# Forty throwaway matmuls in place of forty-seven at the start of a spectral-filter-plus-MLP kernel

## The chip, the cores and the metric

The kernel runs on one core of one Trainium2 chip. The metric is the device time of one execution in microseconds; lower is better. Three runs of the kernel before gave 148.82, 148.93 and 149.20 us, so the median is 148.93 us.

## The reference, cut to what matters

One input `x` of 2048 rows and 640 columns (bf16) is layer-normalised along its columns. The normalised `xn` goes through two branches, and the output is their sum with `x`:

```
xn  = _layernorm(x, axis=-1)
X   = jnp.fft.rfft2(xn, axes=(-2, -1)) * (w_r + 1j * w_i)
y_A = jnp.fft.irfft2(X, s=(2048, 640), axes=(-2, -1))
y_B = gelu(xn @ w1 + b1) @ w2 + b2          # w1 640x1536, w2 1536x640
return x + y_A + y_B
```

## The kernel before, in words

The 2048 rows are cut into 16 row tiles of 128 rows (tile c holds every sixteenth row). Branch B is two layers of matmuls. Branch A is a two-dimensional Fourier transform written as matmuls with constant tables (`gtab`, `etab`, `mtab` and, on the way back, `ntab`, `getab`, `htab`), with foldings on VectorE (DVE) between them and the filter multiplication in the middle.

The program is a list of operations with buffers that they read and write. The order on every engine is written out by hand in the string `ORDER` (`K.arrange(ORDER)`), and `K.sync()` puts in the semaphore waits that the buffers demand. Each engine then runs its own list strictly in order. Neither the string nor the planner's cost estimates are computed again at build time, so a number of matmuls inside one operation can change without moving anything on any engine.

What the first 40 us hold, with the lines of the profile:

- SyncE (SP) issues the loads back to back (L375): row tiles 0 and 1 of `x` one by one, then three chunks of `w1` (into `W1`), `x` tiles 2 and 3, two more chunks of `w1`, the table `gtab`, the other `x` tiles in pairs, and `w2`. None of these issues waits for a compute engine.
- DVE zeroes a 128x128 tile `warm` (L399), and TensorE (PE) multiplies it by itself, writing into a PSUM bank that nobody reads. These are the throwaway matmuls. They are built by `idle(n, ...)` (L411 to L412, recorded under L383), called once with `WARM[0]` matmuls (L413) and once with `WARM[1]` (L532). In `ORDER` both calls stand at the head of PE's list, so they form one unbroken run.
- DVE takes the statistics of a row tile (L480, L482), and ScalarE (ACT, row tile 0, L486) or GpSimd (POOL, all others, L491) makes the reciprocal standard deviation `rstd` from `ve` (L490). DVE then normalises the tile into `T` (L510).
- PE transposes row tiles 0 to 3 against `ident` (L528, five 128x128 transposes each), and DVE (L395) and ACT (L394) copy them out of PSUM into `xnT`. Most later row tiles are transposed by DMAs that SP issues (L519), each of them waiting for DVE's L510.
- Between the transposes PE turns the bias `b1` into a column (twelve one-column matmuls, `ident,gT`) and then runs the first layer of branch B: 24 matmuls with chunks 0 and 1 of `w1` on tile 0, the transposes of tile 1, and so on. ACT applies the GELU (L593, L611).
- DVE folds the normalised tiles for branch A (L540, L544), and PE transforms them with `gtab`.

From then on PE carries the second layer, the Fourier stages and the output, in the order of `ORDER`.

Of the kernel before, what the change touches and what calls it, by code (L numbers as in the profile page):

```python
# [88 lines left out]
def mm_us(n):  # L89
    return max(n / 2400.0 + 0.0027, 0.0265)  # L90
# [6 lines left out]
def act_us(n, ptr=0):  # L97
    return 0.067 + n / 1200.0 + 0.078 * ptr
# [191 lines left out]
AHEAD = 2  # L290
CHAIN = "b0 b1 c00 c01 b2 c10 c11 d00 d01 b3 b4 c20 c21 d10 d11 b5 c30 c31 d20 d21 d30 d31".split()
XASPLIT = [((0, 1, 2, 3, 4),)] * 7 + [((0, 1), (2, 3, 4))]
WARM = (39, 8)
FILTER = {7: 4}


def bass_parallel_sum__spectral_gfnet__dense_activation_gelu__prompt_kernel(
# [21 lines left out]
    with ExitStack() as es:  # L319
# [45 lines left out]
        def psb(slot, dims, off=0, p0=0, n=128):  # L365
            return bass.AP(tensor=PS, offset=p0 * 4096 + slot * 512 + off, ap=[[4096, n]] + dims)
# [20 lines left out]
        def pe(segs, prio, lst, **kw):  # L387

            return K.op([("pe", sum(u for _, u in segs))], prio, mms(lst), segs=segs, **kw)
# [19 lines left out]
        def idle(n, us, **kw):  # L409

            b = Buf("warmps", psum)  # L411
            return pe([("128", us)], 300, lambda: [(psb(b.slot, [[1, 128]]), warm[:], warm[:], True, True) for _ in range(n)], reads=[B_warm], writes=[b], **kw)  # L412
        idle(WARM[0], 0.1067 * 32 + (WARM[0] - 32) * mm_us(128))  # L413

# [80 lines left out]
        for pair in range(8):  # L495
# [10 lines left out]
            for n in range(2):  # L506
# [15 lines left out]
                for j0, j1, engs in ((0, 2, ["dve"]), (2, 5, ["act"])) if c < 2 else ((0, 5, ["dve", "act"]),):  # L522
# [8 lines left out]
                    if j0 and not c:  # L531
                        idle(WARM[1], WARM[1] * mm_us(128), gate=[tp])  # L532
                    us = {"dve": 0.06 + 0.068 * nj, "act": act_us(128 * nj)}
# [287 lines left out]
```

## Time and profile before

| | us |
|---|---|
| median of three runs (148.82 to 149.20) | 148.93 |
| the profiled execution's own time | 149.58 |
| span of that execution, first to last instruction | 147.8 |
| PE busy | 141.9 (96%) |
| DVE busy | 110.0 (74%) |
| ACT busy | 72.3 (49%) |
| POOL busy | 21.5 (15%) |

The profile is of one execution; 149.58 - 147.8 = 1.8 us of its time lie outside the span. A row of a timeline reads: start, duration, engine, line, operation, output and inputs, shape, count, and in brackets the engine's idle time before it with what ended it. PE's matmuls overlap: the spacing of starts within a row of n matmuls is (duration of the row - duration of one) / (n - 1). A row of the chain of waits reads: start, duration, and what the chain was in.

### The profile page before, as it was taken

What the parts mean: (1) busy time and instruction counts of PE and PEld (TensorE: products, weight loads), DVE (VectorE), ACT (ScalarE), POOL (GpSimd) and SP (SyncE); (2) the same over time, 40 slices, a digit from 0 to 9 for tenths busy, and PEclk for the clock granted to TensorE, in tenths of its full rate; (3) what the DMA queues carried; (4) which work ended last, traced back from release to release, by engine and by line L of the source; (5) the groups of instructions that cost most, each with busy time, mean ns of one, the idle gap of its engine ahead of it and who ended that gap; (6) DMA issues with size and microseconds to landing.
All of it is one profiled execution on the core that took longest, in us unless ns stands there. A gap on an engine that the chain in (4) does not pass through costs nothing.

```text
span 147.8 us, 3951 instructions
## 1 busy us (share of the span) xinstructions
PE 141.9 (96%) x1677; PEld 90.5 (61%) x1692; DVE 110.0 (74%) x240; ACT 72.3 (49%) x118; POOL 21.5 (15%) x35
## 2 busy tenths in 40 slices
PE   7999999999799999999999999999999999999993
PEld 7999995655456645445644545555666656655573
DVE  2688999999996367856966979864099787769543
ACT  3615995047598579977775756121075400430000
POOL 1002040301200005000000000000002024545620
DMA  5999999569999998988700670475302107777974
GB/s 119 305 402 399 378 388 132 113 141 135 165 163 160 158 161 218 350 334 45 141 4 0 41 138 10 89 93 106 71 4 24 20 4 84 93 89 91 114 87 114
DMA packets 29843, 21.01 MB, mean 142 GB/s; under 512 B 20225, under 2 KB 27137, under 8 KB 29826
## 3 DMA queue, kind: packets, MB, share of 16 engines
q1 hardware_dynamic: 27232, 15.84, 49.7%
q0 software_dynamic: 2592, 4.92, 17.8%
q8 instruction: 13, 0.21, 0.6%
q14 instruction: 4, 0.03, 0.1%
q10 hardware_dynamic: 2, 0.00, 0.0%
HBM read 13.54 MB, written 5.24 MB: 127 GB/s over the span
## 4 chain that ended last, share of the span: by engine, by line
PE 89%; DVE 5%; DMA 2%; issue 2%; SPq 1%
PE ps L383 88%; DMA xnT<-T 2%; DVE W L780 1%; DVE stats L480 1%; PE ps L528 1%; DVE T L544 1%; DVE T L510 1%; DVE T L540 1%; DVE X L771 1%; SPq L519 1%; DVE mv L482 0%; DVE warm L399 0%; DVE ve L490 0%
## 5 line engine op out<-in xcount | busy, mean ns | idle before, releaser
L383 PE MATMUL ps<-xnT,W 128*128 128x512 bf16 (+2 forms) x336 | 56.9, 320 | 1.0 <-DMA xnT<-T 1.0
L383 PE MATMUL ps<-W,gT 128*128 128x128 bf16 (+3 forms) x382 | 55.0, 292 | 1.5 <-issue 1.0
L383 PEld LDWEIGHTS ps<-W,gT 128*128 128x128 bf16 x396 | 30.1, 98 | 22.5 <-issue 1.7
L383 PEld LDWEIGHTS ps<-xnT,W 128*128 128x128 bf16 x336 | 31.4, 114 | 18.5 <-ACT gT L611 2.8
L611 ACT ACTIVATE gT<-ps,b1col 128x512 bf16<-128x512 f32 (+1 forms) x48 | 28.4, 638 | 15.1 <-PE ps L383 15.1
L787 POOL DMA_DIRECT2D out_dram<-W x14 | 12.3, 990 | 71.0 <-DVE W L780 71.0
L394 ACT ACTIVATE Wf<-ps 128x960 bf16<-128x960 f32 (+1 forms) x10 | 8.5, 888 | 17.9 <-PE ps L383 17.9
L480 DVE BATCH_NORM_STATS2 stats<-X 128x6 f32<-128x320 bf16 x32 | 14.0, 477 | 2.1 <-DMA X<-in_A_x_dram 2.1
L678 DVE TENSOR_TENSOR T<-Y,Wf 128x1288 bf16<-128x1288 bf16 x16 | 12.5, 822 | 0.0
L491 POOL TENSOR_TENSOR rstd<-ve,mhalf 128x2 f32<-128x2 f32 (+1 forms) x8 | 6.0, 744 | 31.9 <-DVE ve L490 31.8
L395 DVE CAST Y<-ps 128x644 bf16<-128x644 f32 x7 | 5.8, 829 | 5.4 <-PE ps L383 5.4
L394 ACT ACTIVATE Xb<-ps 128x960 bf16<-128x960 f32 (+1 forms) x7 | 8.0, 1166 | 3.4 <-PE ps L383 3.3
L544 DVE TENSOR_TENSOR T<-T 128x512 bf16<-128x512 bf16 (+1 forms) x32 | 9.0, 313 | 0.2
L394 ACT ACTIVATE XV<-ps 128x1280 bf16<-128x1280 f32 (+2 forms) x8 | 8.9, 1109 | 0.5 <-PE ps L383 0.5
L395 DVE CAST Xb<-ps 128x960 bf16<-128x960 f32 (+1 forms) x5 | 5.5, 1105 | 4.2 <-PE ps L383 4.2
L394 ACT ACTIVATE Y<-ps 128x644 bf16<-128x644 f32 x9 | 6.3, 708 | 4.1 <-PE ps L383 4.0
L510 DVE TENSOR_SCALAR T<-X,mv,rstd 128x640 bf16<-128x640 bf16 x16 | 6.9, 441 | 1.5 <-POOL rstd L491 1.0
L383 PE MATMUL ps<-getab,XV 32*128 32x160 bf16 (+1 forms) x128 | 7.5, 242 | 0.0
L540 DVE TENSOR_TENSOR T<-T 128x640 bf16<-128x640 bf16 x16 | 7.4, 480 | 0.1
L739 DVE TENSOR_TENSOR Wf<-Wf 128x960 bf16<-128x960 bf16 (+1 forms) x12 | 6.7, 596 | 0.9 <-PE ps L383 0.8
L780 DVE TENSOR_TENSOR W<-ps,b2bc 128x640 bf16<-128x640 f32 x6 | 4.8, 821 | 3.3 <-PE ps L383 3.3
L383 PE MATMUL ps<-etab,XV 32*128 32x160 bf16 (+1 forms) x128 | 7.2, 232 | 0.0
(53 smaller groups left out, 123.1 us busy)
## 6 DMA issues: line engine op xcount, KB each, us to landing
out_dram<-in_A_x_dram POOLq DMA_DIRECT2D x4, 640.0 KB, 7.3
X<-in_A_x_dram SPq DMA_DIRECT2D x7, 320.0 KB, 9.4
out_dram<-W POOLq DMA_DIRECT2D x14, 160.0 KB, 3.4
W<-in_B_w_dram SPq DMA_DIRECT2D x5, 384.0 KB, 5.8
W<-in_B_w_dram SPq DMA_DIRECT2D x3, 640.0 KB, 12.8
Wf<-in_A_w_r_dram SPq DMA_DIRECT2D x7, 160.5 KB, 3.9
Wf<-in_A_w_i_dram SPq DMA_DIRECT2D x7, 160.5 KB, 4.6
gtab<-c_G SPq DMA_DIRECT2D x1, 512.0 KB, 9.1
```

Of the source, the lines that this page charges most:

```text
L383: ins = e.matmul(o_, lhsT=lw, rhs=rh, start=st, stop=sp_, skip_group_check=True)
L394: return e.activation(dst(), src(), ACT.Copy, scale=scale)
L395: return e.tensor_copy(dst(), src())
L480: st_ops.append(K.op([("dve", 0.393)], pr, lambda e, _, c=c, h=h: e.bn_stats(stats[:, c, 6 * h:6 * h + 6], view(X, c * D + H2 * h, [[1, H2 ...
L510: o = K.op([("dve", 0.356)], pr, lambda e, _, c=c, n=n, xnv=xnv: e.tensor_scalar(out=xnv(n, 0, [[1, D]]), in0=view(X, c * D, [[1, D]]), sc ...
L540: K.op([("dve", 0.39)], pr, lambda e, _, k=k, op=op, xnv=xnv, x1v=x1v: e.tensor_tensor(out=x1v(H2 * k, [[D, 2], [1, H2]]), in0=xnv(0, 0, [ ...
L544: ring_ops.append(K.op([("dve", 0.333 if w == 128 else 0.136)], pr, lambda e, _, op=op, x1v=x1v, xfv=xfv, o_=o_, o0=o0, o1=o1, w=w: e.tens ...
L611: K.op([("act", act_us(128 * nt, 1) + 0.02)], pr + PRIO["gelu"], lambda e, _, c0=c0, nt=nt, fc=fc, hps=hps: e.activation(gT[:, fc, 128 * c ...
L678: filt_ops.append(K.op([("dve", 0.738)], pr, lambda e, _, k=k, Y=Y, TB=TB, pair=pair: e.tensor_tensor(out=view(TT, TB.slot * 8 * KP + k * ...
L739: K.op([("dve", 0.068 + n / 6)], pr + 3, lambda e, _, k=k, op=op, y2=y2, yf=yf, n=n: e.tensor_tensor(out=view(Wf, YF + yf.slot * 3 * D + ( ...
L780: K.op([("dve", dve_us(w))], 95, lambda e, _, os_=os_, fps=fps, o0=o0, w=w, xo=xo, base=base: e.tensor_tensor(out=view(W1, OST + os_.slot ...
L787: last.append(K.op([("pool", 0.9)], 450, lambda e, _, c=c, os_=os_: e.dma_start(ov[:, c, :], view(W1, OST + os_.slot * D, [[1, D]]), accum ...
```

## The change

One constant changes: the first `idle` call issues 32 throwaway matmuls and no longer 39. With the 8 of the second call, PE's list begins with 40 of them and no longer 47. On every other engine, and behind the throwaway matmuls on PE, the instructions, their order and their waits are the same.

```
-WARM = (39, 8)
+WARM = (32, 8)
```

## The prediction

> **What bounds the kernel now.** I read the page's chain first, then the chain of waits in order of time, then PE's and DVE's timelines over the first microseconds, then single loads with their time to landing.
>
> The page's chain by engine says that PE sets the end:
>
> ```profile
> PE 89%; DVE 5%; DMA 2%; issue 2%; SPq 1%
> ```
>
> The chain in order of time (start, duration, what) shows where the head of PE's list matters, and where it stops mattering:
>
> ```profile
> 0.99 5.19 PE ps L383 x47
> 6.19 0.53 PE ps L528 x5
> ...
> 22.54 6.50 PE ps L383 x53
> 29.04 0.02 issue
> 29.06 0.07 DVE T L544
> ...
> 35.64 0.80 SPq L519
> 36.44 0.04 issue
> 36.48 2.64 DMA xnT<-T
> 39.12 0.09 issue
> 39.21 23.83 PE ps L383 x268
> ```
>
> The 47 throwaways are its first large piece. At 29.04 it leaves PE for DVE, goes through a DMA transpose, and returns to PE at 39.21, where PE had waited. So what is won early counts only as far as DVE shares it. PE's and DVE's timelines at the head:
>
> ```profile
> 0.99 5.19 PE L383 MATMUL ps<-warm 128*128 128x128 bf16 x47 [0.99 <-DVE warm L399]
> 5.98 0.74 PE L528 MATMUL ps<-ident,T 128*128 128x128 bf16 x5
> 6.65 0.55 PE L383 MATMUL ps<-ident,gT 1*128 1x1 bf16 x12
> 7.13 1.53 PE L383 MATMUL ps<-xnT,W 128*128 128x128 bf16 x24
> 8.50 0.44 PE L528 MATMUL ps<-ident,T 128*128 128x128 bf16 x5
> ```
> ```profile
> 4.72 0.45 DVE L510 TENSOR_SCALAR T<-X,mv,rstd 128x640 bf16<-128x640 bf16 x1
> ```
>
> Tile 0 is normalised at 4.72 + 0.45 = 5.17, but its transposes start at 5.98, right behind the throwaways. One throwaway lasts 0.314 us, so their starts are (5.19 - 0.31) / 46 = 0.106 us apart. The first transposes: (0.74 - 0.31) / 4 = 0.107. The 24 real matmuls, at 0.22 us each: (1.53 - 0.22) / 23 = 0.057. So PE ran at half its rate until between 6.4 and 7.1, the granted clock reading 1.00 throughout. All 47 throwaways ran slow.
>
> **The change, part by part.** *Removed:* 7 x 0.1065 = 0.75 us of PE. Tile 0 becomes usable at 5.17 plus a hand-over of about 0.07 (the DVE copy's signal at 7.06 is followed by PE's row at 7.13), so the transposes start at about 5.25 instead of 5.98: 0.73 us earlier. The 40 slow throwaways end just then, and PE does not idle.
>
> *What follows at once.* DVE waited 0.94 us for these transposes (its copy at 6.75). That copy moves to 6.02, and behind it in DVE's queue the `ve` of tile 1, POOL's `rstd` and the normalising of tile 1 (7.79 to about 7.06). All are 0.73 earlier; nothing else is in their way.
>
> *What stops it on PE.* Loads do not move: SP's issues wait for no compute engine. The first three `w1` chunks are issued at 1.66, 2.13 and 2.61 and land 4.8, 5.3 and 5.8 us later: 6.5, 7.4 and 8.4. PE uses them at 7.13, 7.8 (twelve matmuls further on) and 8.78. With about 0.1 us to pick each up, the lead shrinks to 0.5, 0.3 and 0.28 us. I take 0.28 us for PE from there on.
>
> *What stops it on DVE.* The statistics of tiles 2 and 3, now at 9.42, need a load issued at 3.08 that takes 6.2: it lands at about 9.27, so DVE's lead is at most 0.13 there. DVE idles 0.09 us before its copy at 13.69 and can regain that. Then comes the load that decides: its issue, its landing (last number), and the DVE instruction that needs it, each from its own answer:
>
> ```profile
> 6.68 0.71 SPq L375 DMA_DIRECT2D X<-in_A_x_dram  x1
> ```
> ```profile
> X<-in_A_x_dram SPq DMA_DIRECT2D x1, 320.0 KB, 9.4
> ```
> ```profile
> 16.13 0.49 DVE L480 BATCH_NORM_STATS2 stats<-X 128x6 f32<-128x320 bf16 x1
> ```
>
> 6.68 + 9.4 = 16.1: DVE starts on it as it lands. Whatever lead DVE had is spent, and from 16.1 to 29 it is packed. One hole is left, just where the chain leaves PE:
>
> ```profile
> 28.77 0.14 DVE L490 TENSOR_SCALAR ve<-mv 128x2 f32<-128x2 f32 x1
> 29.06 0.43 DVE L544 TENSOR_TENSOR T<-T 128x512 bf16<-128x512 bf16 x1
> ```
>
> The hole is 29.06 - 28.91 = 0.15 us, and DVE instructions otherwise overlap by a few hundredths, so DVE can start up to about 0.2 us earlier if PE is 0.28 earlier. PE has no wait of its own between 13 and 29 that would eat that lead (it idles 0.05 there). From 29.06 the chain is DVE, SP's issue, the DMA and PE, each waiting for the one before it, so 0.15 to 0.2 goes through to 39.21 and to the end. The lead PE holds beyond it becomes idle time before 39.21, which hides it.
>
> *Sum.* I take -0.18 us: 149.58 to 149.4 for the profiled execution. That one lies 0.65 above the median; carried over, 148.93 - 0.18 = 148.75 us. Bounds: 0 if the hole at 29 does not close, or if PE in other executions speeds up before its throwaways are over and they end earlier anyway; -0.73 if no load were in the way.
>
> *The unknown cost: what the throwaways buy.* The trace shows that PE changes rate after some 5.7 us of nearly unbroken work (0.99 to about 6.7), not what decides the moment. Before, real transposes filled PE to 6.5 with a hole of 0.13. After, they end at 5.8, then twelve one-column matmuls run to about 6.35, then PE idles until chunk 0 has landed and is picked up at about 6.6. If the moment is fixed by time, or the work until 5.8 is enough, this costs nothing. If unbroken work is needed, the fast rate comes later: the second rival.
>
> [...]
>
> [...]
>
> **The rivals.** *Full rate comes later (slower).* Every microsecond at half rate costs PE 1 - 57/107 = 0.47 us of matmuls. PE begins its real matmuls about 0.5 us earlier, so the point of balance is about 1 us of delay, until 7.7. PE's row of transposes at 13.21 feeds DVE's copy at 13.69 with 0.09 us to spare, and behind that DVE is packed up to 35.6, so a late PE passes straight through to the end. If the change needs the same 5.7 us again from 6.6 on, it comes at 12.3, and the loss is 5.6 x 0.47 - 0.5 = 2.1 us; between that and nothing I take the middle, 1.1 us: 150.0 us. For it: PE stayed slow through 5.0 us of unbroken throwaways, so the condition is not met easily, and its new hole of 0.2 to 0.8 us lies just before 6.7. Against it: 4.8 us of unbroken work remain, and weight loads of 0.11 us each fill most of the one-column stretch.
>
> *The whole 0.73 us goes through (faster): 148.2 us.* The landings that stop it are those of one profiled execution, which was 0.65 us slower than the median. If the loads land some tenths earlier otherwise, DVE keeps more of its lead. Against it: the loads keep the DMA engines full in this stretch (9s in the page's slices), and several of them, not one, leave under 0.5 us.
>
> *It does not do what it says.* If PE usually changes rate before the throwaways end, fewer of them are slow and the removed ones cost little: 148.9. That lies within the forecast's case.
>
> **How the numbers follow.** About 0.3% (0.45 us) is what a measurement of this kernel can tell from no change. Forecast: 0.44, at 148.5 to 149.0; all of it counts as the same. Late full rate: 0.36, at 149.4 to 151.0. Full lead: 0.20, at 148.1 to 148.5. So faster 0.20, same 0.44, slower 0.36. The range 148.2 to 150.1 leaves out the upper part of the second case (0.13) and the edge of the third (0.05).
>
> **What would show it.** Right: transposes (L528) at about 5.25, the copy behind them at about 6.0, the 24 matmuls at about 6.6 and still 0.056 apart, DVE's statistics at 16.1 unmoved, the return to PE at about 39.0. Wrong by the second rival: the 24 matmuls 0.107 apart, and DVE's copy at 13.69 and its statistics at 16.13 later by the same amount. Wrong by the third: the statistics at 16.13 earlier.

## The result, and the profile after

The change makes the kernel slower by 0.9%: the ratio of its time to that of the kernel before is 1.0092, with a 95% interval of 1.0064 to 1.0119. That is 148.88 us before (median of six runs) and 149.74, 150.22, 150.53 and 150.59 us after. Left out of all ratios are runs more than 1.5% above the fastest of their kernel: two of the change (152.0 and 152.3 us) and two of e2 below (152.2 and 152.4), each at a mean granted clock of 0.99, one each of e4 (150.6) and e9 (150.8) at 1.00, and one of the kernel before (207.6) at 0.66. The profiled execution took 150.53 us with a span of 148.7, against 149.58 and 147.8 before.

PE's timeline at the head of the kernel after (start, duration, operation, count):

```profile
0.99 4.23 PE L383 MATMUL ps<-warm 128*128 128x128 bf16 x40 [0.99 <-DVE warm L399]
5.28 0.45 PE L528 MATMUL ps<-ident,T 128*128 128x128 bf16 x5
5.66 0.55 PE L383 MATMUL ps<-ident,gT 1*128 1x1 bf16 x12
6.15 0.86 PE L383 MATMUL ps<-xnT,W 128*128 128x128 bf16 x12
7.86 0.86 PE L383 MATMUL ps<-xnT,W 128*128 128x128 bf16 x12 [0.85 <-DMA W<-in_B_w_dram]
8.56 0.44 PE L528 MATMUL ps<-ident,T 128*128 128x128 bf16 x5
```

The transposes start at 5.28, 0.70 us earlier, as planned. Here PE changed to its full rate within the throwaways (at 4.9 us; the transposes are (0.45 - 0.22) / 4 = 0.057 apart), and the matmuls behind are at full rate too. The lead is gone at 7.86, where PE waits for the second `w1` chunk, and at 8.56 PE is 0.06 us behind the kernel before.

DVE's statistics on the load that the prediction called decisive:

```profile
16.16 0.48 DVE L480 BATCH_NORM_STATS2 stats<-X 128x6 f32<-128x320 bf16 x1
```

At 16.16 against 16.13 nothing has moved. But here it was not the load that held DVE: it was issued at 7.24 and landed 8.4 us later, at 15.6, and DVE was busy without a gap until 16.16. From 8.56 to 38 us the new kernel's PE runs 0.06 to 0.09 us behind. Then comes the place where PE waits. Before:

```profile
37.52 0.72 PE L383 MATMUL ps<-gtab,T 128*128 128x128 bf16 x10
39.21 1.89 PE L383 MATMUL ps<-xnT,W 128*128 128x512 bf16 x8 [0.97 <-DMA xnT<-T]
```

After:

```profile
37.59 0.72 PE L383 MATMUL ps<-gtab,T 128*128 128x128 bf16 x10
40.17 1.03 PE L383 MATMUL ps<-xnT,W 128*128 128x512 bf16 x4 [1.86 <-issue]
```

PE comes back at 40.17 instead of 39.21: 0.96 us later, and the span is 0.95 us longer. The whole loss of the profiled execution arises in this one wait. The ratio makes 1.37 us of 148.88; what the other 0.4 us are is not shown. The profiled execution of before lay 0.7 us above its median, so its own wait of 0.97 us may be longer than usual.

What PE waits for is the last of four DMA transposes (L519). SP issued it earlier than before, at 35.62 instead of 36.48, and yet it landed later. SP's queue with the last two of the four transposes, before, and after with the last one by itself:

```profile
34.62 3.15 SPq L519 DMA_TRANSPOSE xnT<-T  x2
```
```profile
34.28 2.61 SPq L519 DMA_TRANSPOSE xnT<-T  x2
```
```profile
35.62 1.28 SPq L519 DMA_TRANSPOSE xnT<-T  x1
```

The last one's row in the list of DMA issues (last number: us from issue to landing), before and after:

```profile
xnT<-T SPq DMA_TRANSPOSE x1, 2.6
```
```profile
xnT<-T SPq DMA_TRANSPOSE x1, 4.5
```

36.48 + 2.64 = 39.12 became 35.62 + 4.46 = 40.08. PE is back 0.09 us after this landing in both. The bracket after the change says "issue", that is, it names no releaser; the times do, since the same 0.09 us lie between the two in e1 to e8 below. After the transpose SP issues the same loads of filter weights in both, beginning 1.3 us behind it (at 37.81 and 36.94). What differs is a line of the list of DMA queues that the prediction did not read. On the page of before it says (packets, MB, share of the 16 engines):

```profile
q8 instruction: 13, 0.21, 0.6%
```

There are 13 packets of 16 KB in the span, and the trace has PE at 1677 matmuls and 1692 weight loads: (1677 + 1692) / 13 = 259 instructions per packet. Counted from the start of the first packet (283 matmuls and weight loads have begun) to that of the last (3195), it is 243. This points to PE's own program, fetched piece by piece as PE goes through it; the page names the queue `instruction` and does not say whose program it carries. The third of these packets starts at 34.28 us before and at 37.79 us after, and the DMA views of 33.9 to 35.9 us of before and of 37.4 to 39.0 us of after each hold it. The first line is the busy share of the DMA engines in 40 slices, in tenths:

```profile
DMA  9971089999999999990000000000001010000000
q8 instruction: 1, 0.02, 3.4%
```
```profile
DMA  9998864119000000000000604459461658699999
q8 instruction: 1, 0.02, 3.6%
```

The packet takes 1.07 us before and 0.92 us after. While it is under way the DMA engines move nothing else for about half a microsecond (34.80 to 35.33 before, 37.80 to 38.24 after). Before, it lies ahead of the last transpose, among the three earlier ones: these land 4.0 to 5.0 us after their issue (2.9 to 3.7 after the change), and SP's issue of the third takes 36.44 - 34.62 = 1.8 us (1.3 after the change). So it seems not to be free there either. After, it lies between issue and landing of the transpose that PE needs. Seven throwaways are fourteen PE instructions (47 matmuls and 47 weight loads on `warm` before, 40 and 40 after), so removing them lets PE reach each point of its list fourteen instructions before its place in the packets of before, and the packets fall later against the rest of the kernel. Fourteen instructions are about 1.5 us here (a matmul of 512 columns with its weight load every 0.216 us); the packet moved by 3.5 us, and what makes up the difference is not shown. All this is a reading of two traces; the experiments test it.

### The profile page after: what moved, and what is told of

Its sections match the earlier page's. It is cut to its first block, busy times and chain, and to the rows that moved or that the text cites. A ratio compares the mean times of both kernels' runs of the same rounds, so it can differ in the third digit from the quotient of the medians.

```text
span 148.7 us, 3952 instructions
## 1 busy us (share of the span) xinstructions
PE 142.6 (96%) x1685; PEld 89.5 (60%) x1685; DVE 109.8 (74%) x240; ACT 72.1 (48%) x118; POOL 21.4 (14%) x35
## 4 chain that ended last, share of the span: by engine, by line
PE 92%; DMA 4%; issue 1%; ACT 1%; SPq 1%; DVE 0%
PE ps L383 91%; DMA W<-in_B_w_dram 4%; ACT gT L611 1%; SPq L375 1%; PE ps L528 1%; DVE W L780 0%
## 5 line engine op out<-in xcount | busy, mean ns | idle before, releaser
L383 PE MATMUL ps<-W,gT 128*128 128x512 bf16 (+3 forms) x396 | 57.4, 295 | 0.0
L611 ACT ACTIVATE gT<-ps,b1col 128x512 bf16<-128x512 f32 (+1 forms) x48 | 28.4, 637 | 16.1 <-PE ps L383 16.0
L544 DVE TENSOR_TENSOR T<-T 128x512 bf16<-128x512 bf16 (+1 forms) x32 | 9.0, 313 | 1.4 <-PE ps L383 1.4
```

The costliest lines, as they stand in the source:

```text
L383: ins = e.matmul(o_, lhsT=lw, rhs=rh, start=st, stop=sp_, skip_group_check=True)
L544: ring_ops.append(K.op([("dve", 0.333 if w == 128 else 0.136)], pr, lambda e, _, op=op, x1v=x1v, xfv=xfv, o_=o_, o0=o0, o1=o1, w=w: e.tens ...
L611: K.op([("act", act_us(128 * nt, 1) + 0.02)], pr + PRIO["gelu"], lambda e, _, c0=c0, nt=nt, fc=fc, hps=hps: e.activation(gT[:, fc, 128 * c ...
```

## The experiments

Theory A: the number of PE instructions at the head decides where the third instruction packet falls; when it falls on the last transpose, that costs about 1 us. Theory B: the length of the throwaway run decides, by clock, loads or the order of the first 16 us. Each kernel was timed in five rounds beside the kernel before.

**Count and length apart (e1, e2).** `cols` is the number of columns that each throwaway multiplies.

```
 e1: WARM = (39, 8), cols = 109      # 47 matmuls, as long as 40
 e2: WARM = (32, 8), cols = 150      # 40 matmuls, as long as 47
```

> 47 throwaway matmuls, each of 109 columns in place of 128: as many PE instructions as before, but together as long as the 40 of the change (47 x 109 = 5123 columns, 40 x 128 = 5120). Theory A (the number of PE instructions ahead of a point sets when the 16 KB packets of the profile's instruction queue fall, and one of them now falls on the DMA transpose that PE waits for at 39 us): as the kernel before, 148.9 us or up to 0.2 less, no instruction packet between 36 and 39.5 us. Theory B (the shorter run of throwaways breaks or delays the early stretch: clock, loads, order of the first 16 us): as the change, 150.0 to 150.6 us.

> 40 throwaway matmuls of 150 columns: as few PE instructions as in the change, but together as long as the 47 of before (6000 against 6016 columns). Theory A: as the change, 150.0 to 150.6 us, with an instruction packet at about 37 to 38 us and PE back from its wait at about 40.2. Theory B: as the kernel before, 148.9 us, PE back at about 39.2.

e1: 148.82 us, ratio 0.9998 (0.9978 to 1.0018). e2: 150.38 us, ratio 1.0070 (1.0031 to 1.0108). PE's timeline in e1, the first transposes and the end of the wait:

```profile
5.28 0.74 PE L528 MATMUL ps<-ident,T 128*128 128x128 bf16 x5
...
38.62 2.54 PE L383 MATMUL ps<-xnT,W 128*128 128x512 bf16 x11 [0.58 <-issue]
```

and in e2:

```profile
5.97 0.74 PE L528 MATMUL ps<-ident,T 128*128 128x128 bf16 x5
...
40.30 0.81 PE L383 MATMUL ps<-xnT,W 128*128 128x512 bf16 x3 [2.06 <-DMA xnT<-T]
```

e1 has the head of the change (transposes at 5.28) and the time of before; e2 has the head of before (5.97) and the late return of the change (40.30). The packet starts at 34.5 in e1 and at 37.2 in e2. The time goes with the count, not with the length: theory B falls. But two of e2's six runs in the ratio, at 148.74 and 149.13 us, were as fast as the kernel before. Only one execution of each kernel has a trace, so whether the packet fell elsewhere in those two is not shown.

**The instructions put back later (e3).** In the matmuls with `gtab` at about 19 us:

```
-            (aps matmuls of tile 0) for j in range(5)],
+            (aps matmuls of tile 0) for j in range(5)] + [one-column matmul into an unused column] * 7,
```

> The change (40 throwaways of 128 columns), and seven matmuls of one column added at about 19 us into an unused PSUM column, so that from there on PE's instruction count is that of before while the first 19 us are those of the change. Theory A: as the kernel before, 148.7 to 149.0 us. Theory B: as the change, 150.0 to 150.6 us. If only the first two instruction packets (at about 12 and 22 us) mattered, it would also be as the change.

149.09 us, just above the expected range, ratio 1.0023 (1.0004 to 1.0042). The packet is back at 34.4 and PE returns at 39.33. So most of the loss is repaired from 19 us on, without touching the head: the first packet, and everything in the first 19 us, cannot be its cause. The 0.2% that remain include the seven added matmuls, which the trace does not separate from the rest.

**More and fewer instructions at equal length (e4, e5, e6, e8).**

```
 e4: WARM = (46, 8), cols = 95       # 54 matmuls
 e5: WARM = (57, 8), cols = 79       # 65
 e6: WARM = (18, 8), cols = 196      # 26
 e8: WARM = (36, 8), cols = 116      # 44
```

> 54 throwaways of 95 columns (5130 columns, as long as the 40 of the change), so PE's instruction count is as much above before as the change's is below. Theory A: the instruction packet that comes at 34 us before comes about 1.5 us earlier, away from the transposes that end at 39: 148.4 to 149.0 us, and not the time of the change. Theory B: as the change, 150.0 to 150.6 us.

> 65 throwaways of 79 columns (5135 columns, as long as the 40 of the change), 18 more PE instruction pairs than before. At 0.216 us for a 512-column matmul the instruction packet of 34.3 us can be asked for 3.9 us earlier, that is among the loads at 30 us and ahead of the four DMA transposes that are under way from 31 to 39. Theory A: packet at 30 to 32 us, PE's wait ending at 38.3 to 38.9 us, time 148.0 to 148.7 us, the best so far; if it falls on a transpose after all, as before. Theory B (only the length of the throwaway run matters): 150.0 to 150.6 us.

> 26 throwaways of 196 columns (5096 columns, as long as the 40 of the change), 21 pairs fewer than before, so the packet can be asked for 4.5 us later than before, at about 39 us. Theory A: packet at 39 us or later, behind the transposes that PE waits for at 39, and before the next ones that PE needs at 49: PE's wait ends at 38.3 to 38.9, time 148.0 to 148.8 us, unless the second packet (22 us before) now meets the first transposes at 26 to 28 us and costs up to 1 us there. It is the test of whether fewer instructions as such are slow, or only the place of the packet: fewer still than the change, and not slower than before. Theory B: 150.0 to 150.6 us.

> 44 throwaways of 116 columns (5104 columns), three pairs fewer than before and four more than the change. Theory A: the packet is asked for 0.65 us later than before; it starts either in the same gap between transposes as before (34.3 to 34.5 us, time 148.6 to 149.0 us) or in the next one (37 to 38 us, time 150.0 to 150.6 us), and the time goes with the place. Theory B: 150.0 to 150.6 us in either case.

| throwaways | third packet starts, us | PE idle in the wait, us | ratio (95%) |
|---|---|---|---|
| 65 (e5) | 33.8 | under 0.25 | 0.9999 (0.9979 to 1.0019) |
| 54 (e4) | 34.3 | 0.74 | 1.0024 (0.9997 to 1.0051) |
| 47 (e1) | 34.5 | 0.58 | 0.9998 (0.9978 to 1.0018) |
| 44 (e8) | 33.6 | under 0.25 | 1.0008 (0.9985 to 1.0031) |
| 40 (e2) | 37.2 | 2.06 | 1.0070 (1.0031 to 1.0108) |
| 26 (e6) | 40.7 | 0.22 | 0.9987 (0.9965 to 1.0008) |

Fewer instructions are not slow as such: 26 are as fast as 47. Only the packet between 37 and 38 us costs more than the intervals can hide; at 34.3 to 34.5 it goes with a wait of 0.6 to 1.0 us in the traces, which the ratios do not show. My expectation for e5 missed: I had the packet at 30 to 32 us, but from 44 to 65 throwaways it always starts at 33.6 to 34.5. It seems to wait for a gap between transposes, so that its place moves in steps; the trace does not say which DMA engine serves it, so this was not shown. e5 (148.80 us, 148.0 to 148.7 expected) did not get faster than before though its wait is nearly gone in the profile, and e4 (149.20 us) came out above its range of 148.4 to 149.0. e4's trace has a second wait, 0.84 us at 59.7, that before does not have; what PE waits for there is not shown.

**The transpose moved, not the packet (e9), and the same for 47 and 26 throwaways (e10, e11).** In `ORDER`, one load of the filter weights is moved behind the two transposes that follow it on SP's queue (e9 with the change's `WARM`):

```
- ... 159s ... 36s ... 172s ... 170s ... 37s
+ ... 159s ... 172s ... 170s 36s ... 37s
```

> The change, and on SP's queue one load of the filter weights (160.5 KB, issued at 33.65 us, 0.6 us of SP's time) moved behind the two DMA transposes that follow it, so that these are issued 0.6 us earlier. PE's instructions stay those of the change, so the instruction packet is asked for at the same point of PE's list. Theory A, where the packet waits for a gap and then holds up what is behind it: the last transpose lands before the packet starts at 37 to 38 us, PE's wait ends at 38 to 39 us and the time is 148.5 to 149.2 us; or the packet slips ahead of the last transpose again and the time stays at 150.0 to 150.6 us, with the packet seen before the landing. If the few instructions themselves were slow for another reason: 150.0 to 150.6 us with the transposes landed early.

> The kernel before with the same swap on SP's queue. The packet starts at 34.3 as before and delays the transposes of 138 to 140 in the same way, but the last one is issued 0.6 us earlier: PE's wait of 1.0 us shrinks by up to 0.6, time 148.3 to 148.9 us. If the wait is set by the packet alone: 148.9 us.

> 26 throwaways of 196 columns with the same swap: the packet comes after the transposes (40.7 us in the run without the swap) and PE no longer waits. Nothing is left to be won at 39 us, so 148.4 to 148.9 us, like the run without the swap.

e9: 148.78 us, ratio 0.9998 (0.9969 to 1.0027). e10: 0.9989 (0.9961 to 1.0016). e11: 0.9985 (0.9965 to 1.0004). In e9 the last transpose is issued at 34.66 and lands at 37.12, ahead of the packet, which still starts at 37.55. Its row and PE's:

```profile
xnT<-T SPq DMA_TRANSPOSE x1, 2.5
```
```profile
37.57 3.40 PE L383 MATMUL ps<-xnT,W 128*128 128x512 bf16 x15
```

PE no longer waits. The change's instruction count, with its packet where it was, costs nothing once the transpose is out of the way. This also rules out that PE stood still in this wait for want of its own instructions: the packet comes about as late as in the change (37.55 against 37.79), and PE runs on. With e1 to e3 this shows the collision from both sides. In e9 the packet meets loads of filter weights and no transpose, and the other DMA traffic goes on: about 300 packets of it start while the packet is under way. The traced executions of e9 (148.13 us) and of before (149.58) lie 0.65 us below and 0.7 above their medians, so the difference of their spans is not what e9 wins. None of the three is faster than the kernel before beyond its interval, and no tried version beats it.

**Does the idle time itself cost (e7)?** Eight 256-column matmuls into unused PSUM columns stand at the beginning of the change's wait:

```
+            + [256-column matmul into unused columns] * 8      # behind the gtab matmuls at 37.6 us
```

> The change, and eight throwaway matmuls of 256 columns (0.87 us) into unused PSUM columns at about 38.2 us, at the beginning of PE's wait. The packet at 37 to 38 us and the transpose that lands at 40.1 stay, so PE's first real matmul stays at about 40.2 and its idle time shrinks from 1.9 to about 1.0 us. Theory A: 149.8 to 150.6 us, and none of its runs shows a granted clock below 1 in the stretch behind the wait, as two of the change's six did (a part of the change's loss is then the half clock that follows an idle time of 2 us). If the idle time has no part in that, reduced clocks appear as often as for the change.

150.23 us, ratio 1.0089 (1.0065 to 1.0113). The transpose still lands late, 4.3 us after its issue, at 39.56, and PE is back at 39.65:

```profile
39.65 1.46 PE L383 MATMUL ps<-xnT,W 128*128 128x512 bf16 x6 [1.11 <-issue]
```

Filling the wait changes nothing in the ratio: what costs is the late landing, as expected. None of its six runs lay above 150.5 us; six are too few to say that the filler prevented the reduced clock.

## Why the prediction was wrong

It gave 148.75 us and put its largest chance, 0.44, on no change; it came out 0.9% slower.

*The removed matmuls.* Right in time: transposes at 5.28 (5.25 forecast). But the part counted only the 0.75 us that they take. That they are also fourteen instructions of PE's list was put at nothing without a reason, and nearly the whole loss came from that: with the fourteen instructions back (e1, e3), the ratio is 0.9998 and 1.0023.

*What stops the lead.* Right that the loads stop it, but not the one called decisive. In the profile of the change the second `w1` chunk landed at 7.8 instead of 7.5, so PE kept no lead at all and the hole at 29 was not closed (L544 at 29.13). The load for the statistics at 16.16 had been there since 15.6. In e1's trace it landed at 15.6 too, so that the statistics began at 15.89, and L544 came at 28.87, 0.19 us earlier: a lead of the size forecast, but only because that load came half a microsecond sooner than in the profile of before. e1 measures this part of the sum alone, the short head without the lost instructions: 0.9998, which holds no change as well as the -0.18 us (0.9988) forecast.

*"From 29.06 the chain is DVE, SP's issue, the DMA and PE ... so 0.15 to 0.2 goes through to 39.21."* This step failed. It took the DMA's 2.64 us as a constant to be shifted. It was 4.46 us after, because an instruction packet now lay in its way, and PE returned at 40.17 and not at about 39.0. The page's line `q8 instruction` was there to be read.

*The late full rate (second rival).* Right sign, and 150.0 us is near the 150.3 us that the measured ratio makes, but that is luck, since the mechanism did not occur: PE was at full rate at 4.9 us, 3.9 us after its first matmul (5.7 before), the 24 matmuls were 0.057 apart, and e1 with an equally short head is not slower. The worry about the hole in PE's work did not come true in any trace: the rate changed at 4.2 to 6.8 us in all of them. With the change's own throwaways it changed at 4.5 us (e9), 4.9 (the change), 5.6 (e3) and only after the transposes, which end at 5.97, in e7. So the throwaways alone do not fix that moment.

*The full lead (third rival).* It would have needed earlier loads. The load at 16.1 did come half a microsecond earlier in e1's trace, and still a head 0.7 us earlier brings less than e1's interval, 0.33 us.

## What to carry to other kernels

Seven matmuls fewer at the head of PE's list went here with an instruction packet at 37.8 us in place of 34.3, and at 37.2 where the run of throwaways was as long as before (e2). When an edit changes the number of instructions ahead of a stage where an engine waits for a DMA, look in the profile for where the instruction queue's packets fall before and after. To tell such a shift from the edit's own effect, keep the count and change the length, then keep the length and change the count.

## What the runs showed of the hardware that I had not expected

One 16 KB instruction packet of about 1 us, 0.6% of the DMA engines' time in all 13 together, went with a DMA transpose, the one that PE waits for at about 39 us, that landed 4.3 to 4.5 us after its issue (the change, e2, e7) instead of 2.5 to 3.0 (all other traces). How the packet holds a transpose up is not shown: the trace does not name the DMA engine that carries it.

PE's granted clock fell to 0.51 after an idle time of 2.06 us. In the trace of e2, an execution of 152.38 us, windows behind its wait, with the busy time of each engine (instructions), the granted clock, the DMA share and GB/s:

```profile
38.00:40.30 2.30, 0.24 (x5) 0.09 (x3) 2.23 (x8) 0.98 (x2) 0.86 (x1) 1.00 0.22 45
40.30:41.00 0.70, 0.70 (x4) 0.39 (x5) 0.66 (x3) 0.00 (x0) 0.00 (x0) 1.00 0.97 172
41.00:44.40 3.40, 3.40 (x10) 1.26 (x9) 2.58 (x8) 1.82 (x2) 0.00 (x0) 0.51 1.20 184
```

and the third of these windows in the kernel before:

```profile
41.00:44.40 3.40, 3.40 (x25) 1.97 (x24) 3.29 (x12) 3.06 (x5) 0.00 (x0) 1.00 1.28 163
```

PE is busy again from 40.30, and the clock drops to half from 41.0 to 44.4 nevertheless: 10 matmuls where there were 25. The clock fell after 2.06 us in this execution, and not after 1.86 us in the profiled execution of the change (1.00 from 40.17 to 46.4). If the wait set the drop off, it cost twice: itself, and about 1.7 us more for the 3.4 us at 0.51 behind it (an estimate: half of 3.4). One trace shows this, and what sets off the drop is not shown.
